# Attention and a feed-forward block on one core: the first three batches re-planned

## The chip, the core and the metric

The kernel runs on one core of a Trainium2 chip. The core has five engines with queues of their own: TensorE (PE, with its weight loads as PEld), VectorE (DVE), ScalarE (ACT), GpSimd (POOL) and SyncE (SP), which issues most of the DMAs. The metric is the device time of one execution in microseconds (us); lower is better.

## What is computed

Eight batches of eight heads, 576 positions, 64 values per head. Causal attention with a bias that is the difference of a running sum of the positive part of `s`, and then a layer norm and a feed-forward block with a residual on the 512 values of each position.

```python
def _attn_ref(q, k, v, s):
    B, H, S, D = q.shape                       # 8, 8, 576, 64
    scores = np.matmul(q, k.transpose(0, 1, 3, 2)) / np.sqrt(D)
    cum = np.cumsum(np.maximum(s, 0.0), axis=-1)
    bias = -(cum[:, :, :, None] - cum[:, :, None, :])
    scores = np.where(causal, -1000000000.0, scores + np.minimum(bias, 0.0))
    attn = softmax(scores)
    return np.matmul(attn, v)

def _moe_ref(x, g_ln, w_ch1, w_ch2):           # x: (8, 576, 512)
    xn = (x - mean(x)) / np.sqrt(var(x) + 1e-06) * g_ln
    return x + np.maximum(xn @ w_ch1, 0.0) @ w_ch2   # 512 -> 2048 -> 512
```

All inputs and the output are float32; the kernel multiplies in bfloat16.

## The kernel before

One Python loop (`for n in range(BH)`) goes over the 64 heads, n = 8 * batch + head, and the order in which the code issues instructions is the order on each engine: there is no scheduler, each engine takes its own instructions in turn and waits for what the next one needs.

**A head.** `scores(b, h)` (matmuls at L282) writes the transposed scores of a head into three PSUM banks named `sa`, `sb` and `sc`, and ACT's exponential (L293) copies each into `er` in SBUF. The causal mask is added on PE for the first ten heads (L290) and cut out of `er` by POOL afterwards (L301). The last corner of 64 positions is done for two heads at once by `scores_d` into a small tile `sd`, with an exponential (L323) and a POOL select (L324). One head later `pv` multiplies `er` with the values `v_bf` (which hold a column of ones, so the sum comes with it) into `pot` (L351), and DVE normalises into `xb` (L359 to L368).

**The score operands.** `kq[0]` and `kq[1]` hold k and q of four heads each, transposed, with four more rows for the bias: the running sum as three bfloat16 parts `c_hi`, `c_mid` and `c_lo`. For batches below `NPE`, `ld_pair` loads k or q of two heads on SP's queue into a staging tile (`st`, six buffers, shared with the values), `cast_pair` makes bfloat16 of it (`kp`, `qp`), and `qk_pair` transposes it on PE (L239) and copies it out of PSUM in halves (L94 on ACT, L96 on DVE); `aug` writes the bias rows of four heads with four small DMAs (L210 to L213). For the other batches `ld_rows`, `cast_rows` (L158) and `tr_rows` load rows, add the bias columns from `cT`, and transpose with a DMA (L168). `bias_rows` makes `cT` once, with 15 transposes on PE (L220) and copies on DVE (L224, L228).

**The layer norm and the feed-forward block.** When a batch's eighth head is out, `ln_stats`, `ln_aggr` (with a power on POOL, `rs`, L397) and `ln_xn` make normalised rows `xn` on DVE (L410), and `ln_tr` transposes them on PE (`trx`, L426) and copies them into `xT` (L431). The block's work is a queue of 32 units for each batch, each of four large matmuls (`mlp1` at L439 with the first weights, `mlp2` at L457 with the second), and `run_units` spreads them between the pieces of the following heads, three or four for each head from head 10 on. `xm` collects the last 64 positions of all batches, and their 32 units and those of the last batch come at the end.

**The weights.** `ld_w1` loads an eighth of the first weights, `cast_w1` (L191) multiplies it with `g_ln` into bfloat16; `ld_w2` and `cast_w2` (L203) do the same for the second weights without the factor. The staging tile `w` has four buffers, so a later load waits for an earlier cast. The function `pre(n)` holds the table of loads and casts by head.

The names used below: a pair is k and q of two heads; a bias group is the four DMAs of one `aug`; `trqk` and `trx` are the PSUM tiles of the two kinds of transposes.

Of the kernel before, what the change touches and what calls it, by code (L numbers as in the profile page):

```python
# [15 lines left out]
P = 128  # L16
# [3 lines left out]
def kernel(  # L20
# [28 lines left out]
    NPE = 2  # L49
# [136 lines left out]
    def cast_w1(i):  # L186
        c, k2 = i // 2, i % 2
        tmp = loaded.pop(("w1", i))
        for u in range(2):
            kd = 2 * k2 + u  # L190
            nc.vector.tensor_scalar_mul(  # L191
                out=w1_bf[:, kd, c * 512 : (c + 1) * 512],
                in0=tmp[:, u, :],
                scalar1=gln[:, kd : kd + 1],
            )
# [35 lines left out]
    def qk_pair(b, j, engs):  # L231
        i = (b * 2 + j // 2) % 2
        hh = (j % 2) * 2
        n = 0
        for x, kind in enumerate("kq"):
# [6 lines left out]
            for u in range(2):  # L242
                copy_on(
                    engs[n],
# [3 lines left out]
                n += 1  # L248
# [131 lines left out]
    def ln_stats(b, part):  # L380
        xs = x_tiles(b)
        if part == 0:
            st[b] = small.tile([P, 5, 2, 6], F32, name="stats", tag="stats", bufs=2)
        lo, hi = (0, 384) if part == 0 else (384, 512)
        for t, x in enumerate(xs):
            nc.vector.bn_stats(out=st[b][:, t, part, :], in_=x[:, lo:hi])
# [132 lines left out]
    nc.scalar.dma_start(out=gln, in_=moe_g_ln.rearrange("(kd p) -> p kd", p=P))  # L519
    nc.gpsimd.memset(kq[0][D : D + 1, 0].bitcast(F32), NEG2)  # L520
    nc.vector.memset(kq[0][D:KA, 1].bitcast(F32), ONE2)
    nc.vector.memset(c_one, 1.0)
    make_identity(nc, ident)
    nc.gpsimd.memset(maskT, 0.0)
# [9 lines left out]
    nc.vector.memset(kq[0][0:KA, 0, :, S:SP], 0.0)  # L534
# [8 lines left out]
    cast_pair("q", 0, 0, "pool")  # L543
# [6 lines left out]
    qk_pair(0, 0, ("act", "dve", "act", "dve"))  # L550
    aug(0, nc.scalar)
# [3 lines left out]
    ld_pair("k", 0, 2)  # L555
    ld_pair("q", 0, 2)
    cast_v(0, 0, "act")
    cast_v(0, 1, "pool")
    ld_pair("k", 0, 3)
    ld_pair("q", 0, 3)  # L560
    for i in range(2):
        nc.gpsimd.memset(v_bf[i][:, 0:NF, :, D : D + 1], 1.0)
        nc.gpsimd.memset(v_bf[i][TL:P, NF, :, :], 0.0)
        nc.gpsimd.memset(v_bf[i][0:TL, NF, :, D : D + 1], 1.0)
    nc.gpsimd.memset(er[TL:P, :, OD : OD + TL], 0.0)
    nc.gpsimd.memset(er[:, :, OD + TL : EW], 0.0)
    cast_v(0, 2, "pool")
    cast_v(0, 3, "pool")
    cast_v(0, 4, "pool")
    nc.gpsimd.memset(kq[1][D : D + 1, 0].bitcast(F32), NEG2)  # L570
    nc.gpsimd.memset(kq[1][D:KA, 1].bitcast(F32), ONE2)
    nc.gpsimd.memset(kq[1][0:KA, 0, :, S:SP], 0.0)
    aug(1, nc.sync)


    def pre(n):
        b, h = n // H, n % H
        if n == 0:
            cast_pair("k", 0, 2, "pool")
            cast_pair("q", 0, 2, "pool")  # L580
            ld_pair("k", 1, 0), ld_pair("q", 1, 0)
            ld_v(1, 0), ld_v(1, 1)
            nc.vector.memset(mhalf, -0.5)
        elif n == 2:
            cast_pair("k", 0, 3, "pool")
            cast_pair("q", 0, 3, "pool")
            ld_v(1, 2), ld_v(1, 3)
            ld_w1(0), ld_w1(1), ld_w1(2), ld_w1(3)
        elif n == 3:
# [4 lines left out]
        elif n == 4:  # L594
            cast_pair("k", 1, 0, "pool")
            cast_pair("q", 1, 0, "pool")
            ld_v(1, 4)
            ld_pair("k", 1, 1)
        elif n == 5:
            cast_v(1, 0, "pool")  # L600
            ld_pair("q", 1, 1)
            bias_rows()
        elif n == 6:
            cast_v(1, 1, "pool")
            cast_v(1, 2, "pool")
            ld_pair("k", 1, 2), ld_pair("q", 1, 2)
        elif n == 7:
            cast_v(1, 3, "pool")
            cast_v(1, 4, "pool")
        elif n == 8:  # L610
            cast_pair("k", 1, 1, "pool")
            cast_pair("q", 1, 1, "pool")
        elif n == 9:
            for i in range(4):
                cast_w1(i)
                ld_w1(4 + i)
        elif n == 10:
            cast_pair("k", 1, 2, "pool")
            cast_pair("q", 1, 2, "pool")
            ld_pair("k", 1, 3), ld_pair("q", 1, 3)  # L620
            cast_w1(4), ld_w2(0)
            cast_w1(5), ld_w2(1)
        elif n == 11:
            cast_w1(6), ld_w2(2)
            cast_w1(7), ld_w2(3)
        elif n == 12:
            cast_pair("k", 1, 3, "pool")
            cast_pair("q", 1, 3, "pool")
            cast_w2(0), ld_w2(4)
            cast_w2(1), ld_w2(5)  # L630
        elif n == 13:
            cast_w2(2), ld_w2(6)
            cast_w2(3), ld_w2(7)
        elif n == 14:
            for i in range(4, 8):
                cast_w2(i)
        lead = {2 * NPE: 1}
        for gam in range(2 * NPE, NG):
            m = n - 4 * gam - lead.get(gam, 0)
# [14 lines left out]
        if n == 14:  # L654
            ld_v(2, 0), ld_v(2, 1)
        elif n == 15:
            cast_v(2, 0, "pool"), cast_v(2, 1, "pool")
            ld_v(2, 2), ld_v(2, 3)
        elif n == 16:
# [91 lines left out]
```

## Time and profile before

| | |
|---|---|
| median of 3 runs | 418.12 us (416.05 to 418.8) |
| the profiled execution's own time | 421.35 us |
| its span in the profile | 419.5 us |
| busy: PE, DVE, ACT, POOL | 366.0, 198.1, 176.5, 172.9 us |
| mean granted clock of PE | 0.945 |

The profile is of one execution, which took 3.2 us more than the median; what is added or taken away below is set against that execution and then carried over to the median. A row of a timeline holds the start, the time to the end of the last of its instructions, the engine, the line of the kernel, the operation, output and inputs with shapes, how many instructions were merged, and in brackets the idle time ahead of it and what ended it. Consecutive matmuls overlap, so how fast PE goes is read from the starts of rows and not from their durations. A row of waits says who waited for whom, the sum, how often and the longest. SPq, ACTq and POOLq are the queues' own instructions, such as the issue of a DMA.

### The profile page before, as it was taken

What the parts mean: (1) busy time and instruction counts of PE and PEld (TensorE: products, weight loads), DVE (VectorE), ACT (ScalarE), POOL (GpSimd) and SP (SyncE); (2) the same over time, 40 slices, a digit from 0 to 9 for tenths busy, and PEclk for the clock granted to TensorE, in tenths of its full rate; (3) what the DMA queues carried; (4) which work ended last, traced back from release to release, by engine and by line L of the source; (5) the groups of instructions that cost most, each with busy time, mean ns of one, the idle gap of its engine ahead of it and who ended that gap; (6) DMA issues with size and microseconds to landing.
All of it is one profiled execution on the core that took longest, in us unless ns stands there. A gap on an engine that the chain in (4) does not pass through costs nothing.

```text
span 419.5 us, 8080 instructions
## 1 busy us (share of the span) xinstructions
PE 366.0 (87%) x2888; PEld 201.7 (48%) x2935; DVE 198.1 (47%) x508; ACT 176.5 (42%) x345; POOL 172.9 (41%) x462
## 2 busy tenths in 40 slices
PE   1468718884899999999999999999999999999995
PEld 1356515442455555555455545555555554444442
DVE  7155687443463465357334744572446357212111
ACT  3444405652227635653474357436633650330510
POOL 4941321675655643556357254726564221000000
PEclk9985666999789999999999999999999999999999
DMA  7698029799989739974997699859966002002013
GB/s 183 172 258 229 3 71 267 229 244 191 214 186 206 161 89 227 192 179 106 209 196 164 142 224 178 182 125 209 187 151 139 2 0 77 25 9 79 14 27 75
DMA packets 165639, 61.05 MB, mean 146 GB/s; under 512 B 153696, under 2 KB 156832, under 8 KB 165600
## 3 DMA queue, kind: packets, MB, share of 16 engines
q1 hardware_dynamic: 165040, 60.52, 62.3%
q8 instruction: 23, 0.38, 0.4%
q14 instruction: 16, 0.13, 0.1%
q10 hardware_dynamic: 560, 0.02, 0.1%
HBM read 36.85 MB, written 9.44 MB: 110 GB/s over the span
## 4 chain that ended last, share of the span: by engine, by line
PE 59%; DVE 12%; DMA 10%; POOL 5%; issue 5%; SPq 4%; ACT 2%; POOLq 0%; ACTq 0%
PE ph L439 22%; PE py L457 19%; PE pot L351 7%; DMA vtmp<-in_v_dram 3%; DMA rowtmp<-in_q_dram 3%; DVE kq L96 3%; PE sc L282 3%; PE sb L282 3%; PE sa L282 3%; DVE xn L410 2%; SPq L168 2%; SPq L146 2%; DMA pairtmp<-in_k_dram 1%; ACT er L293 1%; PE trx L426 1%
## 5 line engine op out<-in xcount | busy, mean ns | idle before, releaser
L457 PE MATMUL py<-w_bf,hT 128*128 128x512 bf16 x554 | 136.6, 384 | 1.9 <-POOL w_bf L203 0.5
L439 PE MATMUL ph<-xT,w_bf 128*128 128x512 bf16 x488 | 120.8, 381 | 4.3 <-ACT hT L449 2.5
L449 ACT ACTIVATE hT<-ph 128x512 bf16<-128x512 f32 x108 | 64.3, 598 | 88.3 <-PE ph L439 88.3
L439 PEld LDWEIGHTS <-w_bf 128*128 128x128 bf16 x576 | 52.0, 98 | 57.1 <-issue 7.8
L457 PEld LDWEIGHTS <-hT 128*128 128x128 bf16 x576 | 52.0, 99 | 50.8 <-issue 3.2
L301 POOL TENSOR_SCALAR_AFFINE_SELECT er<-er 128x128 bf16<-128x128 bf16 x216 | 58.9, 297 | 39.1 <-ACT er L293 39.0
L293 ACT ACTIVATE er<-sa 128x512 bf16<-128x512 f32 x64 | 38.1, 595 | 86.5 <-PE sa L282 56.1
L282 PEld LDWEIGHTS <-kq 68*128 68x128 bf16 x464 | 37.0, 104 | 43.1 <-issue 5.6
L447 DVE TENSOR_SCALAR hT<-ph 128x512 bf16<-128x512 f32 x36 | 24.9, 691 | 69.2 <-PE ph L439 67.8
L158 POOL CAST rows<-rowtmp 128x512 bf16<-128x512 f32 (+1 forms) x60 | 37.0, 616 | 45.2 <-DMA rowtmp<-in_q_dram 41.8
L351 PE MATMUL pot<-v_bf,er 128*128 128x65 bf16 x960 | 48.4, 200 | 4.2 <-POOL v_bf L98 2.1
L351 PEld LDWEIGHTS <-er 128*128 128x128 bf16 x960 | 42.0, 102 | 20.1 <-POOL er L301 5.5
L359 DVE RECIPROCAL rinv<-pot 128x5 f32<-128x5 f32 x64 | 12.3, 193 | 80.6 <-PE pot L351 80.4
L98 POOL CAST v_bf<-vtmp 128x512 bf16<-128x512 f32 (+1 forms) x39 | 23.9, 619 | 47.3 <-DMA vtmp<-in_v_dram 35.2
L293 ACT ACTIVATE er<-sb 128x512 bf16<-128x512 f32 x64 | 38.2, 596 | 5.2 <-PE sb L282 5.2
L293 ACT ACTIVATE er<-sc 128x512 bf16<-128x512 f32 x64 | 38.9, 608 | 0.2
L466 DVE TENSOR_TENSOR yo<-py,xb 128x512 f32<-128x512 f32 x32 | 22.0, 689 | 34.1 <-PE py L457 33.8
L282 PE MATMUL sa<-kq 68*128 68x512 bf16 x64 | 26.9, 420 | 11.8 <-ACT er L293 6.5
L282 PE MATMUL sb<-kq 68*128 68x384 bf16 (+2 forms) x176 | 27.2, 260 | 5.2 <-DMA kq<-rows 5.2
L282 PE MATMUL sc<-kq 68*128 68x256 bf16 (+1 forms) x224 | 28.4, 242 | 0.0
L361 DVE TENSOR_TENSOR xb<-pot,rinv 128x256 f32<-128x256 f32 x64 | 27.2, 424 | 2.2
L426 PE MATMUL trx<-ident,xn 128*128 128x128 bf16 x144 | 14.9, 231 | 10.5 <-DVE kq L96 8.6
(75 smaller groups left out, 274.5 us busy)
## 6 DMA issues: line engine op xcount, KB each, us to landing
vtmp<-in_v_dram SPq DMA_DIRECT2D x32, 256.0 KB, 4.0
out_dram<-yo SPq DMA_DIRECT2D x32, 256.0 KB, 2.2
rowtmp<-in_k_dram SPq DMA_DIRECT2D x48, 128.0 KB, 2.7
rowtmp<-in_q_dram SPq DMA_DIRECT2D x48, 128.0 KB, 3.6
w1tmp<-in_moe_w_ch_dram SPq DMA_DIRECT2D x8, 512.0 KB, 7.8
w2tmp<-in_moe_w_ch_dram SPq DMA_DIRECT2D x8, 512.0 KB, 6.0
pairtmp<-in_k_dram SPq DMA_DIRECT2D x8, 288.0 KB, 3.1
pairtmp<-in_q_dram SPq DMA_DIRECT2D x8, 288.0 KB, 4.4
```

What stands on the lines that cost most here:

```text
L98: nc.gpsimd.tensor_copy(out=out, in_=in_)
L158: nc.gpsimd.tensor_copy(out=r[0:pn, :, :, 0:D], in_=loaded.pop(("rows", gam, t))[0:pn])
L282: nc.tensor.matmul(a[:, c + a0 - q0 : c + a1 - q0], lhsT=k_cols(b, h, kb), rhs=cols, start=True, stop=not (pe_mask and diag),)
L293: nc.scalar.activation(out=e[:, o : o + 512], in_=a, func=ACT.Exp, scale=scale)
L301: nc.gpsimd.affine_select(out=e[:, o : o + P], in_=e[:, o : o + P], compare_op=ALU.is_ge, fill=0.0, base=0, pattern=[[1, P]], channel_mult ...
L351: nc.tensor.matmul(pot[:, t, :], lhsT=e[:, o : o + P], rhs=vv[:, kb, h, :], start=(kb == 0), stop=(kb == last),)
L361: nc.vector.tensor_tensor(out=xb[b][:, :, hs], in0=pot[:, 0:NF, 0:D], in1=rinv[:, 0:NF].unsqueeze(2).to_broadcast([P, NF, D]), op=ALU.mult,)
L439: nc.tensor.matmul(ph, lhsT=w1_bf[:, kd, fb * P : (fb + 1) * P], rhs=xT[:, kd, :], start=(kd == 0), stop=(kd == KD - 1),)
L447: nc.vector.tensor_scalar_max(out=hT[:, fb, :], in0=ph, scalar1=0.0)
L449: nc.scalar.activation(out=hT[:, fb, :], in_=ph, func=ACT.Relu)
L457: nc.tensor.matmul(py[0], lhsT=hT[:, fb, t * P : (t + 1) * P], rhs=w2_bf[:, fb, :], start=(fb == 0), stop=(fb == FB - 1),)
L466: nc.vector.tensor_add(out=yo, in0=py[0], in1=x)
```

## The change

- `NPE` goes from 2 to 3: batch 2 too gets its score operands by pairs and transposes on PE, and the transposing DMAs start with batch 3.
- All bias groups (`aug`) are issued from POOL's queue, the first ahead of POOL's pair casts, the second at head 1 for heads 4 to 7, and four more at heads 4, 8, 12 and 16, each for the four heads that begin four heads later. Before, the first was on ACT's queue and the others on SP's.
- The second weights are no longer staged: four DMAs on POOL's queue, at heads 9 to 12, read float32 and write bfloat16 straight into `w2_bf`. The eight casts on POOL go.
- The casts of the first weights are spread: three eighths on POOL (heads 6 and 10), five on DVE (heads 10 to 12); before, all eight on DVE, four of them at head 9.
- For the first ten heads the order is scores, corner, product of the head before, and then, at even heads, the transposes of the next pair but one head; before, the transposes stood ahead of the scores of an odd head. The copies out of PSUM go by whole tiles, k on DVE and q on ACT or DVE, where before three halves went to DVE and one to ACT. After head 9, the transposes again stand ahead of the scores of odd heads.
- `bias_rows` moves from head 5 to head 14, with the memsets of `cT` and `rows` at head 13.
- The statistics of the layer norm are taken in three parts (after the fourth, sixth and eighth head of a batch) instead of two.
- The value casts of batch 0 all go to POOL, and the edges of the two value buffers are set separately.

The core of the diff:

```diff
-    NPE = 2
+    NPE = 3
...
-    def cast_w1(i):
+    def cast_w1(i, eng):
...
-            nc.vector.tensor_scalar_mul(
+            (nc.vector if eng == "dve" else nc.gpsimd).tensor_scalar_mul(
...
     def ld_w2(i):
-        tmp = wst.tile([P, 2, Dm], F32, name="w2tmp", tag="w")
-        nc.sync.dma_start(out=tmp, in_=w2_r[:, 2 * i : 2 * i + 2, :])
-        loaded["w2", i] = tmp
-
-    def cast_w2(i):
-        nc.gpsimd.tensor_copy(out=w2_bf[:, 2 * i : 2 * i + 2, :], in_=loaded.pop(("w2", i)))
+        nc.gpsimd.dma_start(
+            out=w2_bf[:, 4 * i : 4 * i + 4, :], in_=w2_r[:, 4 * i : 4 * i + 4, :]
+        )
...
-    def qk_pair(b, j, engs):
-        i = (b * 2 + j // 2) % 2
+    def qk_pair(g, k_eng, q_eng):
+        b, j = g // 4, g % 4
+        i = (g // 2) % 2
...
-    qk_pair(0, 0, ("act", "dve", "act", "dve"))
-    aug(0, nc.scalar)
+    aug(0, nc.gpsimd)
+    qk_pair(0, "dve", "act")
...
+        elif n == 10:
+            cast_w1(2, "pool")
+            cast_w1(3, "dve")
+            ld_w1(6), ld_w1(7)
+            ld_w2(1)
...
+        for g in range(6, 4 * NPE):
+            if n == 2 * g - 4 and g >= 8:
+                ld_pair("k", g // 4, g % 4), ld_pair("q", g // 4, g % 4)
+            if n == 2 * g - 2:
+                cast_pair("k", g // 4, g % 4, "pool")
+                cast_pair("q", g // 4, g % 4, "pool")
+        if n % 4 == 0 and 2 <= n // 4 + 1 < 2 * NPE:
+            aug(n // 4 + 1, nc.gpsimd)
...
-        if n == 0:
-            qk_pair(0, 1, ("dve", "dve", "dve", "act"))
-        elif h % 2 == 1 and n > 1 and n + 1 < NPE * H:
-            g = (n + 1) // 2
-            qk_pair(g // 4, g % 4, ("dve", "dve", "dve", "act"))
+        if n < 10:
+            scores(b, h)
+            if n == 9:
+                for t in range(NF):
+                    ln_tr(0, t)
+                queue += batch_units(0)
+            if h % 2 == 0:
+                scores_d(b, h // 2)
+            if pend:
+                pv_next()
+            pend.append((b, h))
+            if n % 2 == 0:
+                g = n // 2 + 1
+                qk_pair(g, "dve", ("act", "dve")[g % 2] if g < 5 else "act")
+            continue
+        if h % 2 == 1 and n + 1 < NPE * H:
+            qk_pair((n + 1) // 2, "dve", "act")
```

Three places where instructions stand differently (the rows name the line in each kernel, the operation, and output and inputs; `x2` is two in a row). First ACT at heads 2 and 3; before:

```order
L293 ACTIVATE er<-sa 128x512
L293 ACTIVATE er<-sb 128x512
L293 ACTIVATE er<-sc 128x512
L323 ACTIVATE er<-sd 64x2x64
L94 COPY kq_106<-trqk 64x576
L293 ACTIVATE er<-sa 128x512
L293 ACTIVATE er<-sb 128x512
```

and after:

```order
L289 ACTIVATE er<-sa 128x512
L289 ACTIVATE er<-sb 128x512
L289 ACTIVATE er<-sc 128x512
L319 ACTIVATE er<-sd 64x2x64
L94 COPY kq_106<-trqk 64x576 x2
L289 ACTIVATE er<-sa 128x512
L289 ACTIVATE er<-sb 128x512
```

Before, one half of q is copied on ACT and the other three halves on DVE; after, both halves of q, and those of k on DVE. The next pair, not in these rows, is copied on DVE alone.

Second, DVE from the statistics of batch 0 (head 8) to the normalising of head 8's product; before:

```order
L386 BN_STATS stats<-xb 128x6 x4
L395 BN_AGGR mv<-stats 128x2 x4
L396 TENSOR_SCALAR rs<-mv 128x4
L410 TENSOR_SCALAR xn<-xb,mv,rs 128x512 x4
L191 TENSOR_SCALAR w_bf<-w1tmp,gln 128x512 x8
L96 COPY kq_105<-trqk 64x576 x3
L359 RECIPROCAL rinv<-pot 128x5
```

and after:

```order
L381 BN_STATS stats<-xb 128x6 x4
L390 BN_AGGR mv<-stats 128x2 x4
L391 TENSOR_SCALAR rs<-mv 128x4
L405 TENSOR_SCALAR xn<-xb,mv,rs 128x512 x4
L96 COPY kq_105<-trqk 64x576 x2
L426 COPY xT<-trx 128x4x128 x4
L355 RECIPROCAL rinv<-pot 128x5
```

The eight casts of the first weights (`w_bf`) left this place, one copy of a pair went to ACT, and the copies of the transposed rows now come ahead of the normalising.

Third, POOL at heads 7 to 9, up to the power of batch 0 and a little beyond; before:

```order
L98 CAST v_bf_104<-vtmp 128x8x64
L98 CAST v_bf_104<-vtmp 64x8x64
L98 CAST kp<-pairtmp 96x2x6x64
L98 CAST qp<-pairtmp 96x2x6x64
L324 AFFINE_SELECT er<-er 64x2x64
L397 TENSOR_TENSOR rs<-rs,mhalf 128x4
```

and after:

```order
L98 CAST qp<-pairtmp 96x2x6x64
L207 DMA kq_106<-c_hi 1x4x576
L208 DMA kq_106<-c_hi 1x4x576
L209 DMA kq_106<-c_mid 1x4x576
L210 DMA kq_106<-c_lo 1x4x576
L320 AFFINE_SELECT er<-er 64x2x64
L392 TENSOR_TENSOR rs<-rs,mhalf 128x4
L98 CAST v_bf_104<-vtmp 64x8x64
L198 DMA w_bf<-in_moe_w_ch_dram 128x4x512
```

A bias group now stands between the pair casts and the corner's select and the power, and the first DMA of the second weights follows.

More of the change, by code (lines that the diff above doesn't have):

```diff
@@ L380, in ln_stats @@
     def ln_stats(b, part):
[L381 removed]
         if part == 0:
[L383 to L385 removed]
+            st[b] = small.tile([P, 5, 3, 6], F32, name="stats", tag="stats", bufs=2)
+        lo, hi = ((0, 256), (256, 384), (384, 512))[part]
+        for t, x in enumerate(x_tiles(b)):
             nc.vector.bn_stats(out=st[b][:, t, part, :], in_=x[:, lo:hi])
@@ L555 @@
     ld_pair("k", 0, 2)
+    for t in range(NT):
+        cast_v(0, t, "pool")
     ld_pair("q", 0, 2)
-    cast_v(0, 0, "act")
-    cast_v(0, 1, "pool")
     ld_pair("k", 0, 3)
     ld_pair("q", 0, 3)
[L561 to L564, printed above, removed]
+    nc.sync.dma_start(out=gln, in_=moe_g_ln.rearrange("(kd p) -> p kd", p=P))
     nc.gpsimd.memset(er[TL:P, :, OD : OD + TL], 0.0)
     nc.gpsimd.memset(er[:, :, OD + TL : EW], 0.0)
[L567 to L573, printed above, removed]
     def pre(n):
```

164 lines of the change are left out of this document (74 added, 90 removed).

## The prediction

> **What bounds the kernel now.** I read the busy time by stretches first, cut at score starts: head 0 (16.43), head 10 (65.18), head 19 (124.32), and the end of the heads (340). Each row gives the stretch, its length, the busy time of each engine, the granted clock, the DMA share and GB/s.
>
> ```profile
> 0.00:16.43 16.43, 2.65 (x24) 1.81 (x25) 10.43 (x16) 4.84 (x7) 9.68 (x25) 1.00 0.78 193
> 16.43:65.18 48.75, 31.04 (x315) 24.00 (x315) 28.98 (x73) 19.36 (x39) 17.05 (x28) 0.69 0.52 143
> 65.18:124.32 59.14, 47.39 (x366) 25.58 (x372) 29.58 (x76) 23.23 (x47) 33.95 (x79) 0.88 0.90 222
> 124.32:340.00 215.68, 211.97 (x1818) 116.91 (x1849) 105.78 (x294) 112.62 (x225) 109.88 (x327) 1.00 0.75 160
> 340.00:419.50 79.50, 72.96 (x373) 33.45 (x377) 23.34 (x52) 16.40 (x28) 2.29 (x5) 0.99 0.13 40
> ```
>
> From 124 on PE is busy 212 of 216 us: what comes later is a fixed amount of PE work, so the end moves by as much as head 19 starts earlier. Before that PE idles 14 + 18 + 12 us, and part of its work runs at half clock. The waits, and the stretch around head 9, say why:
>
> ```profile
> ACT kq L94 <- DVE kq L96: 32.2, 6, 11.7
> PE trx L426 <- DVE kq L96: 8.6, 1, 8.6
> PE sb L282 <- DMA kq<-rows: 5.2, 1, 5.2
> ```
> ```profile
> 48.63 0.46 PE L282 MATMUL sa<-kq 68*128 68x512 bf16 x1 [2.95 <-ACT er L293]
> 51.42 0.20 DVE L359 RECIPROCAL rinv<-pot 128x5 f32<-128x5 f32 x1 [3.39 <-PE pot L351]
> 53.65 1.02 POOL L397 TENSOR_TENSOR rs<-rs,mhalf 128x4 f32<-128x4 f32 x1 [1.95 <-PE pot L351]
> 54.70 2.90 DVE L410 TENSOR_SCALAR xn<-xb,mv,rs 128x512 bf16<-128x512 f32 x4 [1.14 <-POOL rs L397]
> 57.52 3.25 DVE L191 TENSOR_SCALAR w_bf<-w1tmp,gln 128x512 bf16<-128x512 f32 x8
> 60.69 2.29 DVE L96 COPY kq<-trqk 64x576 bf16<-64x576 bf16 x3
> 62.26 0.61 PE L426 MATMUL trx<-ident,xn 128*128 128x128 bf16 x4 [8.57 <-DVE kq L96]
> 63.70 1.69 PE L426 MATMUL trx<-ident,xn 128*128 128x128 bf16 x12 [0.84 <-ACT kq L94]
> 65.18 0.63 PE L282 MATMUL sa<-kq 68*128 68x512 bf16 x1
> ```
>
> ACT's one copy of a pair stands ahead of a head's exponentials and waits for the three copies on DVE; PE then waits for the exponentials to free score banks. At head 9 DVE holds the normalised rows, eight casts of the first weights and the copies in one row, and PE waits behind all of it.
>
> **Part 1, heads 0 and 1.** The durations of one head, at the slow clock, are differences of these starts:
>
> ```profile
> 16.43 0.61 PE L282 MATMUL sa<-kq 68*128 68x512 bf16 x1 [5.06 <-DMA kq<-c_lo]
> 18.24 0.61 PE L282 MATMUL sa<-kq 68*128 68x512 bf16 x1
> 19.93 1.03 PE L351 MATMUL pot<-v_bf,er 128*128 128x65 bf16 x15
> 20.77 0.62 PE L282 MATMUL sa<-kq 68*128 68x512 bf16 x1
> 22.58 1.01 PE L351 MATMUL pot<-v_bf,er 128*128 128x65 bf16 x15
> 23.41 0.67 PE L239 MATMUL trqk<-ident,kp 96*128 96x96 bf16 x6
> 24.35 0.63 PE L282 MATMUL sa<-kq 68*128 68x512 bf16 x1
> ```
> ```profile
> 8.23 1.19 ACTq L210 DMA_DIRECT2D kq<-c_hi  x1
> 12.11 0.58 ACTq L213 DMA_DIRECT2D kq<-c_lo  x1
> 14.29 1.72 POOL L98 CAST v_bf<-vtmp 128x512 bf16<-128x512 f32 x3
> 16.05 1.16 POOL L570 MEMSET kq<- 1x1280 f32 x1
> 18.63 0.82 POOL L98 CAST kp<-pairtmp 96x768 bf16<-96x768 f32 x1
> 20.17 0.29 POOL L324 TENSOR_SCALAR_AFFINE_SELECT er<-er 64x128 bf16<-64x128 bf16 x1
> ```
>
> The last of the four DMAs of the bias rows was issued at 12.11 and held head 0 until 16.43, so 4.3 us from issue to use. GpSimd may issue it as soon as the value exists, before its casts, and head 0 can start some 3 us earlier. That does not carry: the output product of head 0 needs the corner mask, POOL's select at 20.17, which still stands behind the value casts and the memsets of the second score buffer (16.05 to 18.63). Only the two pair casts ahead of it (18.63 to 20.17) now come after, and two small memsets take part back. Between 0 and 1.5 us I take **0.6**: head 2 at 20.2.
>
> **The price of a DMA on POOL** stands in no row. The nearest are ACT's four for the same bytes, 1.19 for the first and 0.58 for the last. ACT, like POOL, also computes. I count one dear and three cheap, 2.9 us for a group, 0.73 each; the ends are 2.3 (all cheap) and 4.8 (all dear).
>
> **Part 2, heads 2 to 7.** On ACT the lone copy in front of each odd head goes, as the rows of ACT in the part on the change show. ACT now copies both halves of q, from a tile that DVE does not touch, and every other pair of this stage has no copy on ACT. So the 32.2 us wait has no cause left. What is late next is PE itself: a pair of heads costs scores 1.81 (20.77 to 22.58), product 0.83, transposes 0.94, scores 1.69 (18.24 to 19.93), product 0.84: 6.1 us. DVE's copies, two or four of 0.76 (2.29 for three), lie under it. POOL has two casts (1.5), a DMA group (2.9) in four heads and value or weight casts, some 5 us in two heads: under PE, with little room. The second bias group is the exception: POOL issues it after 20.2 and two casts, its last DMA near 24.0, used 4.3 later at 28.3, where PE would want head 4 at 26.3: a 2.0 wait. The third and fourth group wait on POOL for the scores of heads 3 and 7; corner masks and casts queue behind them, but they have four heads to land. Three times 6.1 and 2.0 make 20.3 against 27.9 (20.77 to 48.63): **7.6** gained.
>
> **Part 3, heads 8 and 9.** The eight weight casts leave DVE's row; four go to POOL two heads earlier (0.57 each, by the value casts; at most 1.02, by the `rs` row), the rest to heads 10 to 12. The chain from head 8: scores and product 2.64; statistics 2.23 (51.42 to 53.65); POOL's power 1.05; xn 2.9; two copies 1.5; four transposes about 2.1; product 0.84. That is 13.3 against 16.55: **3.2** gained. On POOL four DMAs now stand ahead of the power (`rs`) on which xn waits. Counted up from 20.2, POOL reaches it near 42, before DVE's statistics at 45: hidden, if a DMA is not much dearer.
>
> **Part 4, heads 10 to 18.** The full-clock rates:
>
> ```profile
> 81.41 0.62 PE L351 MATMUL pot<-v_bf,er 128*128 128x65 bf16 x15
> 81.86 1.89 PE L439 MATMUL ph<-xT,w_bf 128*128 128x512 bf16 x7
> 83.59 0.42 PE L239 MATMUL trqk<-ident,kp 96*128 96x96 bf16 x6
> 84.10 0.38 PE L282 MATMUL sa<-kq 68*128 68x512 bf16 x1
> 84.76 1.89 PE L439 MATMUL ph<-xT,w_bf 128*128 128x512 bf16 x8
> 32.50 1.55 PE trc L220 x15
> ```
>
> Product 0.45, two units of the feed-forward 1.73, a pair's transposes 0.51, scores 0.66. PE's work: 32 units 27.7; nine heads at 1.11 and five corners (1.81 less 1.69, halved) 10.3; four pairs 2.0, two of them new; five row transposes 1.2 (63.70 to 65.18 is three at half clock); the bias transposes, moved here, 0.8 (half of 1.55). That is 42.0. The 5.2 us wait on transposing DMAs goes, since these heads no longer use them. The second weights need no cast; their four DMAs take 3 us of POOL (4 x 0.73), which is busy 33.95 of 59.14 us here. Left are a slow clock after the gap at head 9 (about 2: `sa` takes 0.63 at 65.18 and 0.38 at 84.10) and, at head 16, a bias group of 2.9 ahead of the second power (about 2 of it): 46 against 59.1, **13.1** gained.
>
> **Part 5, later.** Two more pairs at 0.51 each: **1.0** lost. The extra split of the statistics is a few short DVE instructions under PE.
>
> Sum: 0.6 + 7.6 + 3.2 + 13.1 - 1.0 = 23.5. The profiled execution took 421.35, with 419.5 of span, and comes out near 398; it was 3.2 above the median, so against 418.12 I predict **395 us**.
>
> **The clock.** Part 2 keeps half clock, on this row of heads 5 to 7, where PE was busy 9.25 of 9.51 us and was granted 0.51:
>
> ```profile
> 36.09:45.60 9.51, 9.25 (x92) 7.24 (x92) 6.03 (x14) 3.96 (x8) 2.94 (x5) 0.51 0.43 112
> ```
>
> The Trainium skill ("TensorE: Matmul & The Clock Gate", What's actually happening) says full speed comes after one busy window of about 3.4 us; by it part 2 would not be PE's, and POOL's 5 us for two heads would give 3.3 us more. This row disagrees with it.
>
> **Rivals.** *POOL's DMAs become the bound (slower).* There are 28 of them, 24 for bias rows and 4 for weights. If all lay on the path, the gain would be used up when each took 0.84 us more than 0.73 (23.5 / 28). POOL does lengthen beside DVE: four masks took 1.62 beside a run of xn, and 1.03 alone.
>
> ```profile
> 115.92 1.62 POOL L301 TENSOR_SCALAR_AFFINE_SELECT er<-er 128x128 bf16<-128x128 bf16 x4
> 116.61 0.54 DVE L410 TENSOR_SCALAR xn<-xm,mv,rs 128x512 bf16<-128x512 f32 x1
> 120.38 1.03 POOL L301 TENSOR_SCALAR_AFFINE_SELECT er<-er 128x128 bf16<-128x128 bf16 x4
> ```
>
> By that factor a DMA takes 1.15, not enough. If each waits out half a run of kq copies (half of 2.29), the sum is 28 x 1.15 = 32 and the time 427. Chance 0.08. The Trainium skill ("SBUF — State Buffer", Who interferes with whom) has such a lock: descriptors built on GpSimd are starved while DVE runs certain modes. No run here shows it yet.
>
> *Loads become the bound.* Part 4 must move 1.05 MB of first weights, 4.2 of second, 2.7 of pairs, 2.0 of values, 0.5 of rows and 1 of output, about 11.4 MB: 51 us at 222 GB/s and 59 at 193, where I allow 46. Longer runs of bytes than in the row loads speak against it. Late by 5 to 13: 400 to 408. Chance 0.25.
>
> *The early stage does not set the end* (within 1%): heads 19 on would have to absorb the gain, but PE is 98% busy there. 414 to 422, chance 0.05.
>
> **How the numbers follow.** The forecast, 386 to 400, has 0.57: at its low end no wait for the second bias group (2.0), no stalls in part 4 (4) and a faster part 2 (3.3); at its high end all DMAs dear (1.9 on each of two groups) and four casts at 1.02. Late loads 0.25, no change 0.05, slower 0.08, and below 386, 0.05. The range 385 to 408 leaves out about 0.2. A measurement here tells 1% from no change: faster 0.87, same 0.05, slower 0.08.
>
> **What would show it.** Right: ACT no longer waits on DVE kq; head 8 starts near 40, head 10 near 54, head 19 near 100, and the stretch after it keeps its 295 us. Wrong: POOL solid with DMA issues while PE waits for masks or casts; the power late at head 8; PE waiting at heads 13 to 15 for the second weights; a wait on the bias DMA at head 4 of much more than 2.

## The result, and the profile after

| | before | after |
|---|---|---|
| median | 417.88 us (4 runs) | 403.08 us (4 runs, 400.28 to 407.22) |
| ratio, with its 95% interval | 1 | 0.9629 (0.9554 to 0.9703) |
| the same kernel in a second session, 6 runs | 417.9 us (11 runs) | 404.62 us (401.31 to 406.71), ratio 0.9686 (0.9645 to 0.9727) |
| profiled execution, span | 421.35 us, 419.5 us | 400.28 us, 398.6 us |
| mean granted clock of PE | 0.945 | 0.974 |

The changed kernel is 13 to 16 us faster. The ratios leave out every run more than 1.5% above the fastest of its kernel: 407.22 here and, further down, 412.90 of the kernel with staged second weights. The two profiled executions differ by 21.1 us, because the one of before was slower than all the runs listed for it and the one of after was the fastest of its four.

Busy time by stretches of the changed kernel, cut at the starts of the same heads (0, 10, 19) and, last, 1.2 us ahead of the start of the last head, where the cut of before lay on that start; columns as in the first view of the prediction:

```profile
0.00:12.23 12.23, 1.32 (x13) 0.93 (x14) 8.26 (x13) 4.42 (x6) 9.34 (x20) 1.00 0.80 198
12.23:50.73 38.50, 26.86 (x311) 20.88 (x312) 26.39 (x63) 20.79 (x41) 36.34 (x53) 0.81 0.95 236
50.73:102.56 51.83, 46.14 (x410) 26.21 (x415) 38.67 (x94) 26.88 (x52) 31.86 (x72) 0.94 0.64 147
102.56:318.50 215.94, 210.59 (x1812) 116.12 (x1842) 110.23 (x321) 114.16 (x228) 111.40 (x327) 1.00 0.76 159
318.50:398.60 80.10, 74.01 (x377) 33.94 (x383) 23.20 (x54) 16.99 (x29) 2.29 (x5) 1.00 0.13 40
```

Heads 0 to 9 take 38.5 us instead of 48.75, heads 10 to 18 51.8 instead of 59.1, and everything from head 19 on is as it was (296.0 us against 295.2). POOL is now busy 36.34 of 38.50 us in heads 0 to 9, but see what PE waits for (waits of the changed kernel: who waited for whom, sum, times, longest):

```profile
ACT kq L94 <- PE trqk L236: 13.0, 7, 4.9
...
PE trx L421 <- DVE kq L96: 6.1, 2, 3.5
...
PE trx L421 <- DVE xn L405: 5.9, 4, 4.0
...
PE sa L278 <- DMA kq<-c_lo: 4.3, 1, 4.3
```

ACT no longer waits for DVE's copies (32.2 us before). PE still waits for them, twice, in front of the transposes of the normalised rows. These and the head starts are in the timeline of the changed kernel (start, time to the end of the last, engine, line, operation, how many, and the wait ahead; the rows of other instructions in between are left out):

```profile
24.54 0.38 PE L278 MATMUL sa<-kq 68*128 68x512 bf16 x1 [0.96 <-DVE xm L364]
...
29.24 6.19 POOL L191 TENSOR_SCALAR w_bf<-w1tmp,gln 128x512 bf16<-128x512 f32 x4
30.59 0.61 PE L278 MATMUL sa<-kq 68*128 68x512 bf16 x1 [1.98 <-DVE kq L96]
...
36.55 0.38 PE L278 MATMUL sa<-kq 68*128 68x512 bf16 x1
...
42.32 4.60 DVE L405 TENSOR_SCALAR xn<-xb,mv,rs 128x512 bf16<-128x512 f32 x4 [1.68 <-POOL rs L392]
43.69 3.69 POOL L191 TENSOR_SCALAR w_bf<-w1tmp,gln 128x512 bf16<-128x512 f32 x2
44.31 0.61 PE L421 MATMUL trx<-ident,xn 128*128 128x128 bf16 x4 [4.02 <-DVE xn L405]
46.84 1.51 DVE L96 COPY kq<-trqk 64x576 bf16<-64x576 bf16 x2
48.41 1.69 PE L421 MATMUL trx<-ident,xn 128*128 128x128 bf16 x12 [3.49 <-DVE kq L96]
50.73 0.62 PE L278 MATMUL sa<-kq 68*128 68x512 bf16 x1
...
88.34 1.21 POOL L392 TENSOR_TENSOR rs<-rs,mhalf 128x5 f32<-128x5 f32 x1 [0.74 <-DVE rs L391]
89.59 1.92 DVE L405 TENSOR_SCALAR xn<-xb,mv,rs 128x512 bf16<-128x512 f32 x4 [1.33 <-POOL rs L392]
91.42 1.05 DVE L405 TENSOR_SCALAR xn<-xm,mv,rs 128x512 bf16<-128x512 f32 x1
92.48 1.52 DVE L96 COPY kq<-trqk 64x576 bf16<-64x576 bf16 x2
94.06 0.38 PE L421 MATMUL trx<-ident,xn 128*128 128x128 bf16 x4 [2.60 <-DVE kq L96]
94.28 0.53 PE L278 MATMUL sa<-kq 68*128 68x512 bf16 x1
...
102.56 0.38 PE L278 MATMUL sa<-kq 68*128 68x512 bf16 x1
```

What the reader is to see: `trqk` and `trx` share two PSUM tiles, with the smaller `sd` and `trc` (all are allocated under the tag `tr`, with two buffers). At head 9 DVE's queue holds `xn` and then the two copies of k. So a `trqk` tile that PE filled long ago stays occupied until 48.35, and the second group of transposes waits 3.49 us, the last 1.5 of them with all four `xn` done (at 46.92). At head 17 the same order costs 2.60 us, and the matmuls behind it are slow (`sa` 0.53, the next ones 0.63, against 0.38 at full clock; the granted clock was 0.62 from 94.06 to 98.50).

### The profile page after: what moved, and what is told of

It is laid out like the page before. It is cut to its first block, busy times and chain, and to the rows that moved or that the text cites. A ratio compares the mean times of both kernels' runs of the same rounds, so it can differ in the third digit from the quotient of the medians.

```text
span 398.6 us, 8139 instructions
## 1 busy us (share of the span) xinstructions
PE 358.9 (90%) x2911; PEld 198.1 (50%) x2959; DVE 206.7 (52%) x543; ACT 183.2 (46%) x356; POOL 191.2 (48%) x476
## 4 chain that ended last, share of the span: by engine, by line
PE 73%; DVE 10%; POOL 5%; DMA 4%; issue 3%; SPq 2%; ACT 1%; POOLq 0%; ACTq 0%
PE ph L434 27%; PE py L452 25%; PE pot L347 7%; PE sa L278 3%; PE sb L278 3%; PE sc L278 3%; DVE xn L405 3%; DMA vtmp<-in_v_dram 2%; PE trx L421 2%; SPq L168 1%; DVE kq L96 1%; PE trqk L236 1%; POOL rs L392 1%; DVE stats L381 1%; SPq L146 1%
## 5 line engine op out<-in xcount | busy, mean ns | idle before, releaser
L452 PE MATMUL py<-w_bf,hT 128*128 128x512 bf16 x548 | 134.4, 381 | 1.5
L297 POOL TENSOR_SCALAR_AFFINE_SELECT er<-er 128x128 bf16<-128x128 bf16 x216 | 60.0, 301 | 37.1 <-ACT er L289 37.0
L278 PEld LDWEIGHTS <-kq 68*128 68x128 bf16 x440 | 34.4, 101 | 33.9 <-POOL v_bf L98 4.5
L347 PEld LDWEIGHTS <-er 128*128 128x128 bf16 x960 | 40.1, 100 | 20.0 <-POOL er L297 6.1
L158 POOL CAST rows<-rowtmp 128x512 bf16<-128x512 f32 (+1 forms) x50 | 30.6, 613 | 36.4 <-DMA rowtmp<-in_q_dram 32.5
L347 PE MATMUL pot<-v_bf,er 128*128 128x65 bf16 x960 | 45.5, 198 | 2.9 <-POOL er L297 2.7
L278 PE MATMUL sc<-kq 68*128 68x256 bf16 (+1 forms) x208 | 27.3, 242 | 0.1
L278 PE MATMUL sb<-kq 68*128 68x64 bf16 (+1 forms) x168 | 26.4, 259 | 0.0
```

Of the source, the lines that this page charges most:

```text
L158: nc.gpsimd.tensor_copy(out=r[0:pn, :, :, 0:D], in_=loaded.pop(("rows", gam, t))[0:pn])
L278: nc.tensor.matmul(a[:, c + a0 - q0 : c + a1 - q0], lhsT=k_cols(b, h, kb), rhs=cols, start=True, stop=not (pe_mask and diag),)
L297: nc.gpsimd.affine_select(out=e[:, o : o + P], in_=e[:, o : o + P], compare_op=ALU.is_ge, fill=0.0, base=0, pattern=[[1, P]], channel_mult ...
L347: nc.tensor.matmul(pot[:, t, :], lhsT=e[:, o : o + P], rhs=vv[:, kb, h, :], start=(kb == 0), stop=(kb == last),)
L452: nc.tensor.matmul(py[0], lhsT=hT[:, fb, t * P : (t + 1) * P], rhs=w2_bf[:, fb, :], start=(fb == 0), stop=(fb == FB - 1),)
```

## The experiments

All kernels below are the changed kernel with one edit, or with two or three of them together where the text says so, and all compute the full result. The profiles are compared by the time from one head's start to another's:

| kernel | heads 0 to 4 | 4 to 9 | 9 to 10 | 10 to 16 | 16 to 17 | 17 to 19 |
|---|---|---|---|---|---|---|
| changed, first profile | 12.31 | 14.69 | 11.50 | 31.50 | 4.28 | 16.05 |
| changed, second profile | 13.25 | 14.70 | 11.55 | 31.62 | 4.28 | 16.05 |
| first-weight casts on DVE | 15.11 | 15.68 | 10.02 | 32.41 | 4.28 | 16.06 |
| two k copies on ACT | 16.62 | 16.82 | 8.37 | 31.34 | 4.28 | 11.79 |
| both | 14.34 | 16.28 | 10.04 | 31.50 | 4.28 | 11.79 |
| bias groups on ACT | 14.27 | 18.81 | 9.49 | 32.37 | 4.29 | 17.31 |
| `NPE` 2 | 16.02 | 19.14 | 10.09 | 30.21 | 9.06 | 11.29 |
| copies by halves | 14.94 | 19.63 | 11.27 | 32.24 | 4.28 | 16.03 |
| old order | 15.13 | 16.82 | 10.15 | 30.89 | 4.28 | 17.50 |
| early second bias group | 11.81 | 15.09 | 11.05 | 31.83 | 4.29 | 16.05 |
| early group, two k copies on ACT | 11.17 | 15.48 | 8.69 | 32.19 | 4.28 | 11.79 |
| the same in the old order | 11.94 | 17.01 | 8.38 | 30.94 | 4.28 | 11.78 |

Differences in time are worked out from the ratios to the kernel before, which share a session: the difference of a kernel's ratio and 0.9686, times 418, with the two intervals' half widths combined as the root of the sum of their squares. All of them lean on 0.9686; with the 0.9629 of the first session in its place, each kernel would stand 2.4 us slower against the changed one.

### The changed kernel again, the casts, and the copies

The two theories of heads 9 and 17: that DVE's k copies hold a PSUM tile (undone by copying them on ACT), and, its rival, that POOL's casts of the first weights lengthen `xn` (undone by casting on DVE).

> The changed kernel once more, unaltered, to see how far its executions and its profile spread. If the profiled execution of 400.28 us was typical, the median comes out near 400 and the ratio to the kernel before near 0.957; if the other executions (401.7 to 407.2) are typical, near 403 and 0.963. Theory C (the clock): slower executions show head 19 at the same place within 1 us but more work at half clock, or a later head 10; theory W (order of arrival): they show longer waits at heads 9 and 17.

The changed kernel, unaltered, took 404.62 us. Its second profile, again of the fastest execution (401.31 us), does not show theory W: the waits at heads 9 and 17 are 3.49 and 2.60 us as before. Head 10 is 1.7 us later, which theory C allows, but not by the clock: head 0 starts 0.7 later and heads 0 to 4 take 0.9 longer, and from head 4 on the stages agree within 0.12.

```diff
-            cast_w1(0, "pool")
-            cast_w1(1, "pool")
+            cast_w1(0, "dve")
+            cast_w1(1, "dve")
...
-            cast_w1(2, "pool")
+            cast_w1(2, "dve")
```

> The three casts of the first weights that the change put on POOL (heads 6 and 10) go to DVE at the same heads. Theory P (POOL and DVE hold each other up): the four normalised rows at head 9 fall from 4.60 us to 2.9, POOL loses 9.9 us of casts, head 10 starts 1.5 to 3 us earlier than 50.7, time 398 to 400 in an execution like the profiled one. Rival K (the pair's copies on DVE keep PE waiting at heads 9 and 17, whoever casts): the waits of 3.49 and 2.60 us stay and the time moves by less than 1 us; DVE at head 6 gets 1.7 us more and may even cost that.

Measured: 404.85 us, ratio 0.969 (0.9652 to 0.9728). Nothing is gained, and the waits for DVE's copies stay (3.46 and 2.61 us). The four `xn` of head 9 take 3.46 us instead of 4.60 and that stage is 1.5 shorter, but heads 4 to 9 and 10 to 16 are about 1 longer each. Heads 0 to 4 are longer too; they lie ahead of the edit and hold a wait of 3.76 for the second bias group, of which more below. That the casts on POOL lengthen `xn` is not shown: the four took 3.56 to 3.68 us in eight kernels below that have these casts on POOL, and 5.10 in the next kernel but one, which has them on DVE.

```diff
-                qk_pair(g, "dve", ("act", "dve")[g % 2] if g < 5 else "act")
+                qk_pair(g, "dve" if g < 5 else "act", ("act", "dve")[g % 2] if g < 5 else "act")
...
-            qk_pair((n + 1) // 2, "dve", "act")
+            qk_pair((n + 1) // 2, "act" if n == 17 else "dve", "act")
```

> The k copies of the pairs at heads 8 and 17 go from DVE to ACT, so that none stands on DVE between the normalised rows and the copies of their transposes. Theory K: the waits of PE for DVE kq (3.49 and 2.60 us) go, PE regains full clock sooner after head 17, and the time falls by 3 to 6 us. Theory P: the rows stay at 4.60 us and PE then waits for them instead, the time falls by 1 to 2 us at most.

Measured: 397.92 us (396.77 to 401.33), ratio 0.9541 (0.9494 to 0.9589): 6.1 us faster than the changed kernel, give or take 2.6. Rows of its timeline at heads 4, 9 and 17:

```profile
22.07 0.52 POOL L210 DMA_DIRECT2D kq<-c_lo  x1
...
28.91 0.59 PE L278 MATMUL sa<-kq 68*128 68x512 bf16 x1 [4.54 <-DMA kq<-c_lo]
...
50.42 0.61 PE L421 MATMUL trx<-ident,xn 128*128 128x128 bf16 x4 [0.49 <-DVE xn L405]
52.46 1.01 PE L421 MATMUL trx<-ident,xn 128*128 128x128 bf16 x8 [1.43 <-DVE xT L426]
54.10 0.62 PE L278 MATMUL sa<-kq 68*128 68x512 bf16 x1
...
93.40 0.40 PE L421 MATMUL trx<-ident,xn 128*128 128x128 bf16 x4 [0.68 <-ACT er L289]
93.64 1.03 PE L452 MATMUL py<-w_bf,hT 128*128 128x512 bf16 x4
94.50 0.39 PE L421 MATMUL trx<-ident,xn 128*128 128x128 bf16 x4
94.72 0.38 PE L278 MATMUL sa<-kq 68*128 68x512 bf16 x1
```

The waits of 3.49 and 2.60 for DVE's copies are gone. Heads 9 to 10 take 3.1 us less. Heads 17 to 19 take 4.26 less, more than the wait of 2.60: the matmuls behind it now run at full clock (`sa` 0.38, not 0.53). The first of the two theories holds. The profiled execution shows something else too, a wait of 4.54 us at head 4.

> Both edits at once. If the two causes are separate, the gains add: 5 to 8 us less than the changed kernel. If one covers the other, no more than the larger of the two.

Both edits together: 399.75 us, ratio 0.956 (0.9512 to 0.9607), no better than the copies alone (0.8 slower, give or take 2.8). Within that, nothing of the rival shows in the time.

### What each part of the change carries

Four parts were undone one at a time.

```diff
-    aug(0, nc.gpsimd)
+    aug(0, nc.scalar)
...
-            aug(1, nc.gpsimd)
+            aug(1, nc.scalar)
...
-            aug(n // 4 + 1, nc.gpsimd)
+            aug(n // 4 + 1, nc.scalar)
```

> All bias groups on ACT's queue instead of POOL's, at the same heads. If POOL's place for them is worth something (POOL 0.52 us for each, first group early), ACT pays 2.3 to 2.9 us of issue for a group ahead of exponentials and head 0 starts 2 to 4 us later: 2 to 5 us slower than the changed kernel's 404.6. Rival: the queue does not matter, since the landing time of about 4 us is the same and other waits cover it: within 2 us, and POOL, freed of 2.1 us a group, gives some back.

Measured: 406.27 us, ratio 0.9714 (0.9685 to 0.9743), slower by 1.2, give or take 2.1: not told apart from nothing. Head 0 starts 0.4 us later, not the 2 to 4 expected. There is no wait for the second bias group at head 4 in its profile, but ACT's exponentials stand behind its own issues (one waits 4.87 us).

```diff
-        nc.gpsimd.dma_start(
-            out=w2_bf[:, 4 * i : 4 * i + 4, :], in_=w2_r[:, 4 * i : 4 * i + 4, :]
-        )
+        tmp = wst.tile([P, 2, Dm], F32, name="w2tmp", tag="w")
+        nc.sync.dma_start(out=tmp, in_=w2_r[:, 2 * i : 2 * i + 2, :])
+        loaded["w2", i] = tmp
+
+    def cast_w2(i):
+        nc.gpsimd.tensor_copy(out=w2_bf[:, 2 * i : 2 * i + 2, :], in_=loaded.pop(("w2", i)))
```

> The second weights as before the change: eight staged loads on SP's queue and eight casts on POOL, at heads 11 to 14; everything else as changed. If the cast in the DMA was worth something, POOL has 8 us more at heads 12 to 14, its masks come late and head 15 starts 2 to 5 us later. Rival: POOL has room there (busy 32 of 52 us), the time stays within 1.5 us of 404.6.

The loads and the casts stand at heads 11 to 14. Measured: 409.10 us (405.76 to 412.90), ratio 0.9758 (0.9713 to 0.9803), slower by 3.0, give or take 2.5. Staging the second weights again costs time, as far as that interval goes. Its profile is of the execution of 412.90 us and is not in the table, so where the time goes is not shown.

```diff
-    NPE = 3
+    NPE = 2
```

> Batch 2 by rows and transposing DMAs again, bias columns transposed at head 5; everything else as changed. By the prediction's part 4 the wait for the transposing DMA at head 16 (5.2 us) returns, with half clock after it, less 3.1 us of pair and bias transposes on PE: 3 to 7 us slower than 404.6. Rival: with the loads moved and POOL freer the rows land in time: within 1.5 us or 2 us faster.

`bias_rows` and its memsets stand early again in this kernel, since batch 2 needs `cT`, and the first rows are loaded a head later. Measured: 404.16 us, ratio 0.9661 (0.9618 to 0.9703): no difference (1.0 faster, give or take 2.5). The stages say why: with transposing DMAs the kernel waits 4.8 us longer at head 16 (9.06 against 4.28) and gets it back at heads 17 to 19 (11.29 against 16.05), where there is no pair to copy in front of the transposes. That balance hangs on the k copy: heads 16 to 19 take 20.35 us here, 20.33 in the changed kernel and 16.07 in the one with the two k copies on ACT. What `NPE` 3 is worth beside that kernel was not run.

```diff
-    def qk_pair(g, k_eng, q_eng):
+    def qk_pair(g, k_eng, q_eng, halves=None):
...
-                    eng,
+                    halves[2 * x + u] if halves else eng,
...
-                qk_pair(g, "dve", ("act", "dve")[g % 2] if g < 5 else "act")
+                qk_pair(g, None, None, ("dve", "dve", "dve", "act"))
```

> In the first ten heads the copies of a pair go by halves again, three on DVE and the last on ACT; order and the rest as changed. By the prediction's part 2 ACT waits for DVE again (20 us or more in sum over heads 2 to 9) and head 8 starts 5 to 8 us later than the 36.6 to 38.3 seen: 4 to 8 us slower than 404.6. Rival: the new order (transposes two heads ahead) hides that wait, and only the order counts: within 1.5 us.

Measured: 410.28 us, ratio 0.9807 (0.9759 to 0.9856), slower by 5.1, give or take 2.7. Its waits have the old row again:

```profile
ACT kq L94 <- DVE kq L96: 23.1, 5, 9.1
```

Heads 4 to 9 take 19.63 us instead of 14.69. So the copies by whole tiles, each tile with one engine, are the largest of the parts that were undone here.

### The spread at head 4

Heads 0 to 4 differ between profiles that have the same instructions there, and so do the times of one kernel (401.31 to 406.71 in one session). Theory: the second bias group, issued at head 1 beside the loads of the first weights and the values, lands at a time that varies.

```diff
+    nc.gpsimd.memset(kq[1][D : D + 1, 0].bitcast(F32), NEG2)
+    nc.gpsimd.memset(kq[1][D:KA, 1].bitcast(F32), ONE2)
+    nc.gpsimd.memset(kq[1][0:KA, 0, :, S:SP], 0.0)
     nc.gpsimd.memset(kq[0][D : D + 1, 0].bitcast(F32), NEG2)
...
-    v_edges(0)
...
     cast_pair("q", 0, 1, "pool")
+    v_edges(0)
...
     nc.gpsimd.memset(er[:, :, OD + TL : EW], 0.0)
+    aug(1, nc.gpsimd)
...
-            nc.gpsimd.memset(kq[1][D : D + 1, 0].bitcast(F32), NEG2)
-            nc.gpsimd.memset(kq[1][D:KA, 1].bitcast(F32), ONE2)
-            nc.gpsimd.memset(kq[1][0:KA, 0, :, S:SP], 0.0)
...
-            aug(1, nc.gpsimd)
```

> The second bias group is issued on POOL before head 0's masks (about 15 to 17 us) instead of at head 1 (19.3 to 21.3), its constant rows being set in POOL's idle time before. Theory that its landing (3.8 to 7 us after the last issue, beside the w1 and v loads) is what makes head 4 late and the runs of the changed kernel spread: it lands by 24, PE has no wait for c_lo at head 4, heads 0 to 4 take 12 to 12.5 in every run (13.3 to 16.6 before), heads 0 to 9 take 27 rather than 28 to 33, and the time falls by 2 to 4, to 400.5 to 402.5. Rival, that the spread has another source (the clock of heads 2 to 9, the loads): the wait goes and another one follows at head 5 or 6, and the time is within 1.5 of 404.6.

Measured: 399.87 us, ratio 0.9576 (0.953 to 0.9621), faster by 4.6, give or take 2.6, and the four runs lie within 2.2 us (398.59 to 400.76). Head 4 and the group's last issue in the second profile of the changed kernel:

```profile
20.85 0.52 POOL L210 DMA_DIRECT2D kq<-c_lo  x1
...
26.15 0.38 PE L278 MATMUL sa<-kq 68*128 68x512 bf16 x1 [2.93 <-DMA kq<-c_lo]
```

and in the kernel with the early group:

```profile
16.92 0.52 POOL L210 DMA_DIRECT2D kq<-c_lo  x1
...
23.69 0.38 PE L278 MATMUL sa<-kq 68*128 68x512 bf16 x1 [0.20 <-ACT er L289]
```

Head 4 waited 2.93 and 4.54 us in the two profiles of late groups shown here and does not wait for the group now. Of the nine profiles with this group on POOL at head 1, eight show the wait, 2.50 to 4.81 us long, and only the first profile of the changed kernel does not; none of the three with the early group does. The theory holds for the wait and for the time. For the spread it is open: four runs are few, the last kernel below has the early group and spreads by 3.7 us over six runs, and the kernel before, whose profile has no such wait at head 4, spreads by 5.3 over eleven. Which of the loads makes the group late was not tried.

> Early second bias group and the k copies of heads 9 and 17 on ACT together. If the two gains are apart in place and add: 397.9 less 2 to 4, 394 to 396. If the time before head 9 is set by something else: 397 to 399.

With the early group and the two k copies on ACT: 393.92 us (393.48 to 395.18), ratio 0.9449 (0.9416 to 0.9483). The gains add within their intervals: 9.9 us, give or take 2.2, below the changed kernel, against 4.6 and 6.1 of the two alone. This is one of the two fastest kernels of the study, 23 us faster than the kernel before. Its stretches to heads 0, 10 and 19:

```profile
0.00:12.07 12.07, 1.32 (x12) 0.93 (x13) 7.51 (x13) 4.42 (x6) 10.55 (x22) 1.00 0.82 204
12.07:47.41 35.34, 26.59 (x312) 20.70 (x312) 23.82 (x61) 22.06 (x43) 32.76 (x49) 0.82 0.95 242
47.41:95.67 48.26, 45.17 (x410) 25.88 (x415) 37.02 (x92) 28.11 (x54) 32.63 (x73) 0.96 0.65 156
```

### Scores first, or transposes first

```diff
+            if n == 0:
+                qk_pair(1, "dve", "dve")
+            elif n % 2 == 1 and n > 1:
+                g = (n + 1) // 2
+                qk_pair(g, "dve", ("act", "dve")[g % 2] if g < 5 else "act")
             scores(b, h)
...
-            if n % 2 == 0:
-                g = n // 2 + 1
-                qk_pair(g, "dve", ("act", "dve")[g % 2] if g < 5 else "act")
```

> The transposes and copies of the next pair stand ahead of a head's scores again in the first ten heads, all else as in the changed kernel. Theory that this order carries the gain of heads 2 to 8 and, with the k copy on ACT's path, part of heads 9 and 10: heads 0 to 9 take 31 to 33 rather than 27 to 28 and the time rises by 3 to 6, to 408 to 411. Rival, that the earlier bias rows and the copies split by whole tiles carry it: within 1.5 of 404.6.

Measured: 404.97 us, ratio 0.9715 (0.9666 to 0.9764): 1.2 slower, give or take 2.7. The expected 408 to 411 did not come. But head 4 waited 4.2 us for the bias group in its profile, which could hide the order's worth, so the order was tried once more in the kernel without that wait:

> The early second bias group and the k copies of heads 9 and 17 on ACT, but the next pair's transposes and copies ahead of a head's scores again in the first ten heads. The wait at head 4 that hid the order's worth in the profile of the kernel with the old order alone is gone here. Theory that scores first is worth something once head 4 does not wait: heads 0 to 9 take 29 to 32 rather than 26.7 and the ratio to the kernel before is 0.952 to 0.962 (0.945 with scores first). Rival, that the order is worth nothing and only the spread of engines counts: heads 0 to 9 take 26 to 28, ratio 0.942 to 0.948.

Measured: 393.65 us, ratio 0.9451 (0.9405 to 0.9496), against 0.9449 with scores first: a difference of 0.1, give or take 2.4. In the profiles heads 0 to 9 take 2.3 us longer in the old order (28.95 against 26.65), and heads 9 to 16 take 1.6 less (39.32 against 40.88). In the time this part of the change is worth nothing that these runs can tell.

## Why the prediction came out as it did

The forecast of 395 us was 8 us too low. The sign and the range (385 to 408) held, the forecast's own range (386 to 400) did not. The time fell where the range had been widened for late loads, and these did not come, so that the range held was luck. By its own steps, in the profiled executions:

| step | predicted | measured |
|---|---|---|
| part 1, to head 2 | 0.6 | 2.86 (17.91 against 20.77) |
| part 2, heads 2 to 7 | 7.6 | 9.2 (18.64 us against 27.86) |
| part 3, heads 8 and 9 | 3.2 | 2.4 (14.18 us against 16.55) |
| part 4, heads 10 to 18 | 13.1 | 7.3 (51.83 us against 59.14) |
| part 5, from head 19 on | -1.0 | -0.9 (296.0 us against 295.2 in span) |
| sum | 23.5 | 20.9 |

The sum is nearer than its terms: parts 1 and 2 gained 3.9 more than predicted, parts 3 and 4 gained 6.6 less.

**Part 4 is the step that failed**, and in it the last sentence: what is "left" over 42.0 us of PE work, "a slow clock after the gap at head 9" and "a bias group of 2.9 ahead of the second power", together 4. The stage took 9.8 over 42.0. The second power was not held by a bias group: POOL had been idle for 0.74 us when DVE's row for it was done, and started it at 88.34. What held PE was DVE's copy of k between `xn` and the tile that PE needs, and the half clock after it; moving that copy to ACT takes 4.26 us off heads 17 to 19. The prediction had that order at head 9, where it counted two copies in the chain, and did not ask where the same code stands in front of the next layer norm. The PE work itself was also counted too low. An estimate, by busy time and granted clock: of the 46.14 us that PE was busy, 2.9 are the price of slow clock (1.2 behind head 9, where it was 0.50 to 53.00 and 0.90 to 55.00; 1.7 behind the wait at head 17, where it was 0.58 to 96.00 and 0.64 to 98.50), and 43.2 are left as work at full clock; the kernel with the early group and the two k copies on ACT gives 43.2 too (45.17 less 2.0, at 0.50 to 51.00 and 0.87 to 53.00). The pair of transposes in front of head 19, which the prediction counted in part 5, is about 0.5 of the difference to 42.0. The other 5.7 us PE was idle, 3.3 of them in front of the transposes at head 17.

**The carrying over to the median** is the second thing that failed. The prediction took 3.2 us off because the profiled execution of before lay above its median. That assumes the next profile lies as far above. It lay 2.8 below. The 2.4 us by which the sum was too large for the executions' own times (23.5 against 21.1), the 2.8 and the 3.2 make up the 8, but for the rounding to 395. One thing that varies is head 4 waiting, or not, for the second bias group: the first profiled execution of the changed kernel is the one without the wait. How much of the spread it makes is not shown.

**Part 2** named that wait, 2.0 us for the second bias group, from a landing of 4.3 us. In the second profile it was 2.93, with 26.15 - 21.37 = 4.8 us from the end of the last issue to use; in that with the k copies on ACT 4.54, after 28.91 - 22.59 = 6.3. The mechanism was right, the size mostly too small, and in the first profiled execution it was nothing; in the second the part gained 8.1 (19.72 us). That ACT's wait of 32.2 us has no cause left was right, and the copies by halves, with which it came back at 23.1, cost about 5 us; the order of transposes and scores, which the prediction took with it, is worth nothing that the runs can tell.

**Part 1** was too small: POOL's corner mask ran at 17.46 instead of 20.17. Besides the two pair casts that the prediction counted, the memsets of the values' edges (11.74 to 13.64 before) left the place ahead of it, one set for POOL's idle time at 6.24 and one for head 2; one more value cast took 0.5 back. The mask then did not hold PE: head 0 started 4.2 us earlier, at 12.23, and from there to head 2 PE had one wait, of 0.25.

**Part 3** was near in size, by errors on both sides. The casts of the first weights on POOL were priced 0.57 each, at most 1.02, by the value casts; they took 1.55 (6.19 for four) and beside `xn` 1.85 (3.69 for two). `xn` took 4.60 instead of 2.9. The bias group ahead of the power was not wholly hidden: DVE's row was done at 40.64, and POOL started at 41.23. Against that head 8 was at full clock (`sa` 0.38 at 36.55).

**The price of a DMA on POOL**, 0.73 each by estimate, was a little high for the bias rows: a group took 2.1 to 2.4 us against 2.9, most of its DMAs 0.52 and the dearest 0.81. A piece of the second weights took 0.76 to 0.84.

**The clock.** Part 2 kept half clock only in part: heads 4 and 5 ran at full speed, then came a wait of 1.98 us and this row, heads 6 and 7, and at 36.55 full speed again:

```profile
30.59:36.55 5.96, 5.96 (x63) 4.70 (x64) 4.53 (x13) 3.99 (x8) 5.96 (x7) 0.52 1.05 305
```

PE was busy for 6 us without a break at a granted 0.52 before it sped up. The Trainium skill ("TensorE: Matmul & The Clock Gate", What's actually happening) has full speed after about 3.4 us of sustained work: the return came, later than by that rule, while in the kernel before it did not come in 9.5 us. Nor did it come sooner in the second profile of the changed kernel, where PE was granted 0.50 from 28.46 to 38.30, busy for 9.28 of these 9.84 us.

**The rivals.** POOL's DMAs did not become the bound: none took over 0.84 us in the first profile of the changed kernel. Late loads in part 4 were given 400 to 408, and the time lies there, but not for that reason: the DMA share in heads 10 to 18 is 0.64, and PE has no wait for the second weights. Loads may have a price in heads 0 to 4, where the share is about 1 (1.07 from 12.23 to 21.50) and the second bias group is mostly late; which load does it is open. That the early stage does not set the end was wrong: heads 19 on took 296.0 us.

**What the runs give in sum.** Undone one at a time, whole-tile copies are worth 5.1, the second weights' DMAs 3.0, the bias groups on POOL 1.2, the order 1.2 (0 in the faster kernel), `NPE` 3 nothing and the casts on POOL nothing. That adds to some 10 of 13 us, but each has about 2.5 either way, and since all lean on one ratio the sum has about 8. The earlier first bias group, which belongs to the 2.9 of part 1, was not undone alone, and neither were the value casts, the move of `bias_rows` and the statistics in three parts.

## What to carry to other kernels

Where transposes of several kinds share few PSUM tiles, look at what stands in the emptying engine's queue ahead of the copy: a copy that is itself short keeps a tile occupied for as long as the long work in front of it. A small DMA that a stage waits for is issued well before the stage and the bulk loads, not when its turn comes, and several profiles of one kernel are compared to see whether its landing varies. And where a profile is carried over to a median, it is asked what varies between runs, since two profiled executions can lie at opposite ends of it.

## What the hardware showed that I had not expected

- A wait of PE can cost more than itself. Moving one copy took 4.26 us off heads 17 to 19, where the wait was 2.60 and the matmuls behind it took 0.63 in place of 0.38. It need not: at head 9 a wait of 3.49 less made the stage 3.1 shorter, and `sa` behind it stayed at 0.62. Whether the wait of 1.98 brought the half clock of heads 6 and 7 (the row above) was not tried; in the second profile half clock set in at 28.46, behind a wait of 0.48.
- The float32 to bfloat16 multiplication on DVE (`xn`) and POOL's work beside it lengthen each other. Four `xn` took 1.92 us at head 17, 2.90 at head 9 of the kernel before and 3.46 to 5.10 at head 9 of the kernels here; POOL's casts of the first weights took 1.55 each before `xn` and 1.85 beside it. The longest single ones stood beside DMA issues on POOL: the first `xn` took 1.93 (42.32 to 44.25, an issue at 42.80) and, in the kernel with both edits, 3.22 (46.12 to 49.34, two issues from 46.61 to 48.22, none of these casts on POOL), against 0.53 for the shortest. But beside such an issue it also took 1.07, with the two k copies on ACT, so what decides it is open. The Trainium skill ("SBUF — State Buffer", Who interferes with whom) has such operations of DVE and GpSimd exclude each other, whichever comes first; these longer times agree with that. It also has GpSimd's building of descriptors starved by them, and that did not show in the length of the issues: POOL's DMA issue at 42.80, beside `xn`, took 0.84 us, and the four of the second weights took 0.76 to 0.84.
- The landing of the same small DMA, from the end of its issue to use, took 2.5 us for the first bias group (9.71 to 12.23, at a DMA share of 0.73). For the second one it took at most 3.2 in the first profile (share 0.93) and 4.8 and 6.3 in the two others shown (shares 1.04 and 1.02).
